# Other constants and another picking rule in the planner that orders the instructions of an attention and MLP kernel

## The chip, the cores and the metric

The kernel runs on one core of a Trainium2 chip. Its time is the device time of one execution in microseconds (us). Before the change the median of three runs is 223.51 us (223.31 to 223.61). The profile comes from one further execution.

The core has five engines, each with an instruction queue of its own that it works off strictly in order: TensorE (PE, matmuls; its weight loads are listed as PEld), VectorE (DVE), ScalarE (ACT), GpSimd (POOL) and SyncE (SP, which here only issues DMAs). Engines wait for each other and for DMAs through semaphores. An instruction whose wait is not met holds up everything behind it in the same queue.

## The reference, cut to what matters

The first half is a blocked linear attention with decay per head; the second is a two-layer MLP over its output.

```python
# q, k, v: (4, 8, 768, 64); block = 64; rel = pos[:, None] - pos[None, :]
Dmask = where(rel >= 0, lam ** rel, 0)
for b in range(12):
    intra = (qb @ kb.T * Dmask) @ vb
    inter = (qb * lam ** (pos + 1)) @ kv_state
    out[b] = intra + inter
    kv_state = lam ** 64 * kv_state + (kb * lam ** (63 - pos)).T @ vb
x = out.transpose(0, 2, 1, 3).reshape(3072, 512)
h = x @ w_in                          # (3072, 2048)
g = h + sin(alpha * h) ** 2 / (alpha + 1e-9)
y = g @ w_out                         # (3072, 512), float32
```

## The kernel before, in words

**Attention.** The kernel works in 24 blocks of 128 rows (6 per batch entry, all 8 heads at once). For each block, queries, keys and values are loaded as float32: `load_q` (L345) loads q for two blocks, 512 KB, and `load_kv` (L358) loads k and v for one, 256 KB each. The decay is folded into q and k by a multiplication that also casts to bfloat16 (`scale_block`, L458: q at L464, k at L471, on POOL except for the first two k), and v is cast at L473, on ACT, from block 12 on on ACT or POOL. q and k are then transposed. For blocks 0 to 11 TensorE does it (`piece_Q` L496 and `piece_T` L476, with copies out of PSUM at L511 and L493 on DVE or ACT). From block 12 on SP issues a DMA transpose (L479). The scores (`part_S`, matmuls at L543) go through a masking multiplication on DVE (L552) into `Sm`; the state (`part_Z`, L568) is copied out at L578 or L583; the output (`part_O`, L603, L616, L623) is copied into `xT` at L632. `piece_G` (L649) packs scores of one block and output and state of the block before it into one piece of TensorE work.

**MLP.** Rows go in 6 chunks of 512, which is four blocks. For a chunk, 16 units A (`unit_A`, L656, matmuls at L671; or `unit_A2`, L694, L705, which takes half the rows and two column groups) each fill one PSUM bank, then ACT takes the sine (L681, L715), POOL or ACT squares it (L686/L720 or L685/L719), and DVE combines both into `gT` (L688, L723). Only then is the bank free. 16 units B (`unit_B`, L729, L736) multiply `gT` with the second weights; the last of each four is copied out by ACT (L749) and stored (L751). Units A rotate over three banks in most of the kernel.

**Loads.** SP issues, in program order: q, k and v of blocks 0 to 3, the first quarter of the first weights (`load_w1_first`), and then, after the third quarter of the first weights has landed, q, k and v for blocks 4 and up; stores and transposes stand between them. POOL issues the other three quarters of the first weights and four quarters of the second. Loads reuse rings of six buffers for k and v and three for q.

**What sets the order.** The program does not issue instructions directly. Every piece is handed to `_Plan.op` (L54) with the engine or the choice of engines that can do it, a duration in us, what it reads and writes, and for DMAs a time on the wire (`dur`), a time for the issue and a time `lat` after the transfer. `_Plan` finds dependencies, and `_order` (L119) simulates the kernel with these numbers: it picks one piece after another and writes down the order in which each engine gets its pieces; where there is a choice, the engine that would be done first gets it. SP keeps program order. On PE any of the next 40 pieces in program order may be picked; among those that could start within 0.3 us of the earliest (`SLACK`), the one that stands first in the program is taken. ACT, DVE and POOL take what can start first. Work that depends on another engine is taken to be ready 0.2 us after it (`LAT`), an engine is occupied for a piece's whole duration, and a DMA begins to move data 0.8 us after its issue. `_transfers` (L75) shares the wire between the DMA queues; `_settle` (L101) repeats both up to eight times and keeps the pass whose landings agree best. `P.lead` (40 in `attend`, -20 in `run`) moves a piece's place in the program. `P.filler` (L836) puts matmuls without a result (`spin`, L826, L829) into planned gaps of TensorE before the first unit A. The result is a fixed instruction list with semaphore waits; nothing is planned at run time.

Of the kernel before, what the change touches and what calls it, by code (L numbers as in the profile page):

```python
# [13 lines left out]
class _Op:  # L14


    def __init__(self, eng, emit, dur, reads, writes, dma, after, issue, lat, runs=64):
        self.eng, self.emit, self.dur = eng, emit, dur
        self.given = eng
        self.issue, self.lat, self.runs = issue, lat, runs  # L20
        self.lead = 0
# [11 lines left out]
class _Plan:  # L33

    AHEAD = {"PE": 40, "SP": 1}
    SLACK = 0.3  # L40
    EARLY = 0.0, 0.0

    LAT = 0.2
# [10 lines left out]
    def op(self, eng, emit, dur, reads=(), writes=(), dma=None, after=(), issue=0.4, lat=2.6, runs=64):  # L54
# [20 lines left out]
    def _transfers(order):  # L75
# [5 lines left out]
        left = {e: [[o.start + 0.8, o.runs, o.dur / o.runs, o] for o in sorted(q, key=lambda o: o.start)]  # L81
# [19 lines left out]
    def _settle(self):  # L101

        filler, lands, best = self.filler, {}, None
        for _ in range(8):
            self.filler = filler
            for o in self.ops:
                o.eng, o.start, o.done = o.given, None, None
            order = self._order(lands)
            new = self._transfers(order)
            off = sum(abs(t - o.done) for o, t in new.items())  # L110
            state = [(o, o.eng, o.start, o.done) for o in order]
            if best is None or off < best[0]:
                best = off, order, state
            lands = new
        for o, eng, start, done in best[2]:
            o.eng, o.start, o.done = eng, start, done
        return best[1]

    def _order(self, lands):  # L119
        index = {o: i - o.lead for i, o in enumerate(self.ops)}  # L120
        left = {}
        for o in self.ops:
            left.setdefault(o.eng if isinstance(o.eng, str) else "any", []).append(o)
        fixed = {e: left.pop(e, []) for e in ("PE", "SP")}
        free = [o for e in left for o in left[e]]
        clock = {e: 0.8 for e in ("PE", "SP", "ACT", "DVE", "POOL")}
        wire = 0.0
        port = 0.0
        order = []

        def ready(o):
            t = 0.0
            for d in o.deps:
                if d.done is None:
                    return None
                t = max(t, d.done + (0.0 if d.eng == o.eng else self.LAT))
            return t

        while fixed["PE"] or fixed["SP"] or free:
            best = None  # L140
            for e in ("PE", "SP"):
                can = []
                for o in fixed[e][:self.AHEAD[e]]:
                    r = ready(o)
                    if r is not None:
                        can.append((max(r, clock[e]), index[o], o, e, o.dur))
                if can:
                    soon = min(c[0] for c in can)
                    soon += self.EARLY[1] if e == "PE" and soon < self.EARLY[0] else self.SLACK
                    c = min((c for c in can if c[0] <= soon), key=lambda c: c[1])  # L150
                    if best is None or c[:2] < best[:2]:
                        best = c
            for o in free:
                r = ready(o)
                if r is None:
                    continue
                if o.port:
                    r = max(r, port)
                if isinstance(o.eng, str):
                    c = (max(r, clock[o.eng]), index[o], o, o.eng, o.dur)  # L160
                else:
                    _, e, d = min((max(r, clock[e]) + d + late, e, d) for e, d, late in o.eng)
                    c = (max(r, clock[e]), index[o], o, e, d)
# [766 lines left out]
```

## Time and profile before

| what | value |
|---|---|
| median of three runs | 223.51 us |
| the profiled execution | 223.52 us |
| its span, first to last instruction | 221.4 us |
| TensorE busy | 208.6 us (94%) |
| ScalarE busy | 155.9 us (70%) |
| VectorE busy | 122.6 us (55%) |
| GpSimd busy | 89.1 us (40%) |
| HBM read / written | 27.28 / 6.29 MB |
| first unit A starts on TensorE | 19.89 us |

How to read it: busy time is the union of an engine's instructions. Matmuls are pipelined, so the listed duration of one (379 ns at 512 columns) is longer than the step from one to the next (0.216 us), and a short stall after a matmul is partly hidden in its listed duration. "idle before, releaser" says how long an engine stood still ahead of an instruction, and what ended that. The chain of waits follows the last instruction back to what released it, step by step.

### The profile page before, as it was taken

To read this page: it belongs to the slowest core of one execution; us is meant where nothing else is said; L and a number is where in the kernel's file an instruction comes from. 1 tells how busy PE (TensorE), PEld (TensorE's weight loads), DVE (VectorE), ACT (ScalarE), POOL (GpSimd) and SP (SyncE) were. 2 spreads that over 40 slices of the span, in tenths; PEclk is the share of its full clock that TensorE was granted. 3 is DMA by queue.
4 is the path that set the end of the run, shared out by engine and by line. 5 is a ranking of instruction groups with operands and counts; after the bars stand their busy time and mean duration, and the time that the engine had idled before them with its cause. 6 is when DMAs were issued, how large, how long until landed. Compare 5 with 4: busy or idle time off the path is not lost.

```text
span 221.4 us, 4062 instructions
## 1 busy us (share of the span) xinstructions
PE 208.6 (94%) x1645; PEld 110.7 (50%) x1645; DVE 122.6 (55%) x184; ACT 155.9 (70%) x277; POOL 89.1 (40%) x100
## 2 busy tenths in 40 slices
PE   3889987899898999999999999999999999999995
PEld 1446433456575785545445444545545444444444
DVE  4687775354777887667655455645465544445100
ACT  3735994347697997788788887877788677778211
POOL 4386763454978776863576103011001011110100
DMA  5999999999999999999999752110110011101112
GB/s 131 236 232 271 206 214 208 217 235 237 233 245 275 242 191 245 219 254 189 276 240 245 155 112 33 47 50 0 47 50 21 26 47 50 47 0 49 75 70 95
DMA packets 83651, 33.31 MB, mean 150 GB/s; under 512 B 63520, under 2 KB 80688, under 8 KB 83632
## 3 DMA queue, kind: packets, MB, share of 16 engines
q1 hardware_dynamic: 76880, 24.25, 53.6%
q0 software_dynamic: 3696, 3.67, 9.9%
q10 hardware_dynamic: 3056, 5.13, 6.4%
q8 instruction: 13, 0.21, 0.4%
q14 instruction: 6, 0.05, 0.1%
HBM read 27.28 MB, written 6.29 MB: 152 GB/s over the span
## 4 chain that ended last, share of the span: by engine, by line
PE 63%; DMA 24%; POOL 4%; SPq 4%; ACT 2%; DVE 1%; issue 1%
PE bank L736 32%; PE bank L671 24%; DMA k<-in_k_dram 10%; DMA q<-in_q_dram 5%; DMA v<-in_v_dram 4%; DMA w<-in_moe_w_in_dram 4%; SPq L342 4%; PE bank L705 3%; PE bank L623 2%; PE bank L543 2%; POOL qk L471 1%; POOL qk L464 1%; PE bank L603 1%; POOL u L720 1%; DVE gT L723 1%
## 5 line engine op out<-in xcount | busy, mean ns | idle before, releaser
L736 PE MATMUL bank<-w,gT 128*128 128x512 bf16 (+1 forms) x400 | 94.8, 371 | 0.0
L688 DVE SCALAR_TENSOR_TENSOR gT<-u,rinv,bank 128x512 bf16<-128x512 bf16 x74 | 54.6, 746 | 51.7 <-ACT u L685 34.2
L671 PE MATMUL bank<-xT,w 128*128 128x512 bf16 x296 | 74.2, 379 | 0.6 <-DVE gT L688 0.6
L681 ACT ACTIVATE t<-bank,alpha 128x512 bf16<-128x512 f32 x74 | 50.6, 686 | 24.1 <-PE bank L671 24.0
L736 PEld LDWEIGHTS bank<-w,gT 128*128 128x128 bf16 x400 | 37.7, 98 | 39.6
L686 POOL TENSOR_TENSOR u<-t 128x512 bf16<-128x512 bf16 x19 | 19.7, 1040 | 80.7 <-ACT t L681 79.7
L671 PEld LDWEIGHTS bank<-xT,w 128*128 128x128 bf16 x296 | 28.5, 98 | 34.9 <-DVE gT L688 1.1
L685 ACT ACTIVATE u<-t 128x512 bf16<-128x512 bf16 x55 | 34.4, 629 | 1.8 <-DVE gT L723 0.3
L552 DVE TENSOR_TENSOR Sm<-bank,mask 128x1024 bf16<-128x1024 f32 x24 | 29.2, 1222 | 10.3 <-PE bank L568 7.7
L464 POOL TENSOR_TENSOR qk<-q,Lq 128x512 bf16<-128x512 f32 x24 | 24.5, 1044 | 21.7 <-DMA q<-in_q_dram 18.1
L471 POOL TENSOR_TENSOR qk<-k,Lk 128x512 bf16<-128x512 f32 x22 | 22.9, 1044 | 7.2 <-DMA k<-in_k_dram 7.0
L749 ACT COPY osb<-bank 128x512 f32<-128x512 f32 (+1 forms) x25 | 14.2, 569 | 14.8 <-PE bank L736 14.8
L705 PE MATMUL bank<-xT,w 128*128 128x256 bf16 x176 | 22.3, 273 | 2.0 <-DVE gT L723 2.0
L723 DVE SCALAR_TENSOR_TENSOR gT<-u,rinv,bank 128x256 bf16<-128x256 bf16 x44 | 19.1, 476 | 7.2 <-POOL u L720 4.1
L715 ACT ACTIVATE t<-bank,alpha 128x256 bf16<-128x256 f32 x44 | 18.5, 471 | 3.3 <-PE bank L705 3.1
L705 PEld LDWEIGHTS bank<-xT,w 128*128 128x128 bf16 x176 | 16.2, 98 | 5.5 <-DVE gT L723 3.0
L473 ACT CAST v<-v 128x512 bf16<-128x512 f32 x18 | 11.0, 615 | 7.6 <-DMA v<-in_v_dram 7.6
L632 ACT CAST xT<-bank 128x512 bf16<-128x512 f32 (+1 forms) x18 | 12.9, 716 | 2.8 <-PE bank L568 1.6
L720 POOL TENSOR_TENSOR u<-t 128x512 bf16<-128x512 bf16 x11 | 11.3, 1039 | 4.7 <-ACT t L715 4.6
L543 PE MATMUL bank<-qkT 64*128 64x128 bf16 x192 | 9.8, 226 | 0.2 <-DVE qkT L493 0.2
L623 PE MATMUL bank<-Sm,v 128*64 128x128 bf16 x192 | 9.9, 225 | 0.0
L829 PE MATMUL bank<-mask,ident 128*128 128x512 bf16 x12 | 5.7, 564 | 3.7 <-DVE mask L429 3.7
(55 smaller groups left out, 111.4 us busy)
## 6 DMA issues: line engine op xcount, KB each, us to landing
k<-in_k_dram SPq DMA_DIRECT2D x24, 256.0 KB, 5.5
v<-in_v_dram SPq DMA_DIRECT2D x24, 256.0 KB, 5.5
q<-in_q_dram SPq DMA_DIRECT2D x10, 512.0 KB, 5.5
out_dram<-osb ACTq DMA_DIRECT2D x19, 256.0 KB, 2.0
w<-in_moe_w_out_dram POOLq DMA_DIRECT2D x4, 512.0 KB, 13.1
w<-in_moe_w_in_dram POOLq DMA_DIRECT2D x3, 512.0 KB, 9.0
q<-in_q_dram SPq DMA_DIRECT2D x4, 256.0 KB, 4.6
ws<-in_moe_w_in_dram SPq DMA_DIRECT2D x2, 512.0 KB, 5.4
```

The lines of the kernel that those rows point to most:

```text
L464: lambda e, a=a: e.tensor_tensor(qk2[:, j:j + 2, 4 * a:4 * a + 4, :], q32[jq][:, 4 * a:4 * a + 4, :, :].rearrange("p h t d -> p t h d"), b ...
L471: lambda e: e.tensor_tensor(qk2[:, j, H:2 * H, :], k32[jl][:, :, :], lk, ALU.mult), 0.7 if s in (0,1) else 1.05,
L552: op("DVE", lambda e: e.tensor_tensor(Sm[s % 2][:, :, :], banks[:, 512 * b0:512 * b0 + 1024].rearrange("p (c i) -> p c i", i=128), mask[:, ...
L671: ins = e.matmul(ps[hb][:, c0:c1], w1[:, kc, 128 * m:128 * (m + 1)], xT[x][:, kc, c0:c1], start=(kc == 0 and c0 == lo), stop=(kc == NKC - ...
L681: op("ACT", lambda e: e.activation(t16[ju][:, w], ps[hb][:, w], ACTF.Sin, scale=alpha[:, m:m + 1]), 0.69 * f, [bank(hb), "alpha"], [("t16" ...
L685: lambda e: (e.activation(u16[ju][:, w], t16[ju][:, w], ACTF.Square) if e is nc.scalar else e.tensor_tensor(u16[ju][:, w], t16[ju][:, w], ...
L686: e.tensor_tensor(u16[ju][:, w], t16[ju][:, w], t16[ju][:, w], ALU.mult)), 0,
L688: op("DVE", lambda e: e.scalar_tensor_tensor(out=gT[g][:, m, w], in0=u16[ju][:, w], scalar=rinv[:, m:m + 1], in1=ps[hb][:, w], op0=ALU.mul ...
L705: ins = e.matmul(ps[hb][:, 256 * i:256 * i + 256], w1[:, kc, 128 * (m + i):128 * (m + i + 1)], xT[x][:, kc, lo:lo + 256], start=(kc == 0 a ...
L715: op("ACT", lambda e, i=i: e.activation(t16[ju][:, 256 * i:256 * i + 256], ps[hb][:, 256 * i:256 * i + 256], ACTF.Sin, scale=alpha[:, m + ...
L723: op("DVE", lambda e, i=i: e.scalar_tensor_tensor(out=gT[g][:, m + i, lo:lo + 256], in0=u16[ju][:, 256 * i:256 * i + 256], scalar=rinv[:, ...
L736: ins = e.matmul(ps[ob][:, w], gT[g][:, m, 128 * s4:128 * (s4 + 1)], w2[:, m, w], start=(m == 0), stop=(m == NM - 1),)
```

## The change

The planner's model and its rule for picking are replaced; what is computed, the tiles, the buffers and the program order of the pieces stay, but for one load that is named below.

- A hand-over between engines costs `HOP` of the receiving engine (0.035 to 0.1 us), plus `DRAIN` 0.085 us where TensorE is the giver, in place of 0.2 us. ACT, DVE and POOL are free for the next piece `PIPE` (0.11, 0.09, 0.045 us) before the piece is done.
- A DMA begins to move data 2.0 us (POOL: 2.9 us) after its issue instead of 0.8 us, and the time after the transfer falls (mostly to 1.25 or 1.4 us; 2.7 us stays for q, k and v from block 4 on).
- Durations of pieces are set anew, most by a few hundredths of a us; the DMA transpose from 2.5 to 1.0 us, the cast of v on POOL from 1.05 to 0.62 us.
- On PE, ACT, DVE and POOL the planner first finds the earliest start of any ready piece of the engine, and takes the one that stands first in the program among those within a window (PE 0.3 us, the others 0.1 us). Then it takes the engine with the earliest pick.
- Up to ten passes, and the loop ends when landings agree within 0.5 us in sum. `MOVES`, a list of shifts in the program order, is empty.
- The loads of blocks 10 and 11 are asked for in `prep(8)` and `prep(9)` instead of right after `prep(5)`. Between these two places nothing else is handed to SP, so that SP's order is the same.

The hunks stand in the order of the planner's class and then the kernel: the constants, when a piece is ready, the pick, the end of a piece, `load_q`, `load_kv`, the cast of v, the DMA transpose, `piece_T` (`piece_Q` changes likewise), `prep`, and the place after `prep(5)`.

```diff
-    AHEAD = {"PE": 40, "SP": 1}
-    SLACK = 0.3
-    EARLY = 0.0, 0.0
-    LAT = 0.2
+        self.lag = 2.9 if eng == "POOL" else 2.0
+    AHEAD = 40
+    WINDOW = {"PE": 0.3, "ACT": 0.1, "DVE": 0.1, "POOL": 0.1}
+    PIPE = {"ACT": 0.11, "DVE": 0.09, "POOL": 0.045, "PE": 0.0}
+    HOP = {"PE": 0.055, "ACT": 0.035, "DVE": 0.035, "POOL": 0.075, "SP": 0.1}
+    DRAIN = 0.085
+    MOVES = ()
...
+        def ready(o, e):
+            t = clock[e]
+            for d in o.deps:
+                if d.eng == e and (e == "PE" or d.dma is not None):
+                    t = max(t, d.done)
+                else:
+                    t = max(t, d.done + self.HOP[e] + (self.DRAIN if d.eng == "PE" else 0.0))
+            return t
...
+            for e, c in per.items():
+                if not c:
                     continue
+                soon = min(x[0] for x in c) + self.WINDOW.get(e, 0.0)
+                x = min((x for x in c if x[0] <= soon), key=lambda x: x[1])
+                if best is None or x[0] < best[0]:
+                    best = x[0], x[2], e, x[3]
...
-                o.done = max(t + 0.8 + o.dur + o.lat, lands[o]) if o in lands else wire + o.lat
+                o.done = max(t + o.lag + o.dur + o.lat, lands[o]) if o in lands else wire + o.lat
             else:
-                clock[e] = o.done = t + dur
+                o.done = t + dur
+                clock[e] = o.done - self.PIPE[e]
...
-                        (0.9 if s == 0 else 1.1 if s < 4 else 2.3), f"q32{j}" + (str(lo) if s < 4 else ""),
-                        lat=2.7, after=after, runs=8 * (hi - lo),
+                        (0.93 if s < 4 else 2.0), f"q32{j}" + (str(lo) if s < 4 else ""),
+                        lat=1.25 if s < 4 else 2.7, after=after, runs=8 * (hi - lo),
...
-                            (nm, j), 1.1, f"{nm}{j}", lat=2.7,
+                            (nm, j), 1.18, f"{nm}{j}", lat=1.25 if s < 4 else 2.7,
...
-                op((("ACT", 0.62, 0.0), ("POOL", 1.05, 0.3)) if s > 11 else "ACT", lambda e: (e.copy if e is nc.scalar else e.tensor_copy)(v2[j][:, :, :], v32[jl][:, :, :]), 0.62,
+                op((("ACT", 0.62, 0.0), ("POOL", 0.62, 0.3)) if s > 11 else "ACT", lambda e: (e.copy if e is nc.scalar else e.tensor_copy)(v2[j][:, :, :], v32[jl][:, :, :]), 0.62,
...
-                        qkT[:, jt, :, :], qk2[:, j, :, :].rearrange("p a b -> p (a b)")), 2.5,
+                        qkT[:, jt, :, :], qk2[:, j, :, :].rearrange("p a b -> p (a b)")), 1.0,
...
-                op("PE", mm, 0.35, [("k2", j), "ident"], [bank(tb)])
+                op("PE", mm, 0.35 if s < 4 else 0.24, [("k2", j), "ident"], [bank(tb)])
...
-                    for ahead in range(s + 2, min(s + 3, NBLK)) if s >= 10 else ():
+                    for ahead in range(s + 2, min(s + 3, NBLK)) if s >= 8 else ():
...
             prep(5)
-            load_pair(10)
```

## The prediction

> **What bounds the kernel now.** I read the page first, then busy time by stretch, then what TensorE waits for, then the timeline around each of its stalls, last the chain of waits.
>
> Rows 1 and 2 of the page:
>
> ```profile
> PE 208.6 (94%) x1645; PEld 110.7 (50%) x1645; DVE 122.6 (55%) x184; ACT 155.9 (70%) x277; POOL 89.1 (40%) x100
> ...
> PE   3889987899898999999999999999999999999995
> ...
> DMA  5999999999999999999999752110110011101112
> ```
>
> TensorE is full from about 40% of the span on; before that its slices have holes, while the DMA engines are full from about 6 us to about 116 us. Busy time by stretch says how large the holes are (the figures after the stretch are its length, then busy PE, PEld, DVE, ACT, POOL):
>
> ```profile
> 20.00:36.00 16.00, 15.43 (x86) 7.57 (x86) 10.80 (x18) 14.17 (x25) 9.80 (x11) 1.00 1.22 210
> 36.00:60.00 24.00, 21.27 (x211) 12.22 (x210) 11.96 (x18) 11.83 (x24) 12.98 (x13) 1.00 1.08 226
> 60.00:86.00 26.00, 24.80 (x305) 17.50 (x304) 20.83 (x41) 22.52 (x51) 20.32 (x22) 1.00 1.08 233
> 86.00:120.00 34.00, 33.93 (x285) 17.66 (x283) 21.57 (x32) 27.91 (x50) 20.27 (x21) 1.00 1.22 246
> 120.00:204.00 84.00, 84.00 (x526) 40.18 (x525) 42.28 (x56) 65.47 (x107) 12.21 (x13) 1.00 0.20 52
> ```
>
> From 86 us to the last matmul an order can hardly win anything. The waits of PE name the holes (the first row is the start, before any data):
>
> ```profile
> PE bank L829 <- DVE mask L429: 3.7, 1, 3.7
> PE bank L506 <- POOL qk L464: 2.1, 2, 1.7
> PE bank L705 <- DVE gT L723: 2.0, 3, 1.0
> PE bank L488 <- POOL qk L471: 0.7, 2, 0.5
> PE bank L671 <- DVE gT L688: 0.6, 1, 0.6
> ```
>
> The timeline shows what each hides: start, duration, engine and line, and in brackets the idle time before.
>
> ```profile
> 35.70 1.89 PE L736 MATMUL bank<-w,gT 128*128 128x512 bf16 x8
> 39.31 0.40 PE L506 MATMUL bank<-ident,qk 128*128 128x128 bf16 x4 [1.72 <-POOL qk L464]
> 39.55 1.03 PE L671 MATMUL bank<-xT,w 128*128 128x512 bf16 x4
> ...
> 40.63 2.75 PE L736 MATMUL bank<-w,gT 128*128 128x512 bf16 x12
> ...
> 57.16 0.62 ACT L473 CAST v<-v 128x512 bf16<-128x512 f32 x1 [1.69 <-DMA v<-in_v_dram]
> ```
>
> At 0.216 us a matmul, the eight from 35.70 end at 37.43, so TensorE lost 1.88 us to 39.31, with finished work (an A unit and three B units) behind the waiting transpose. At 57.16 ACT stands 1.69 us in front of a cast whose v has not landed; the Square at 57.68 behind it comes late, DVE's `gT` with it, and TensorE's A unit starts at 59.27, 0.88 late. The chain of waits has the same pattern at 85 us:
>
> ```profile
> 72.04 6.72 DMA q<-in_q_dram
> ...
> 78.83 0.92 POOL qk L464
> ...
> 82.43 2.01 POOL u L720 x2
> ...
> 84.46 0.88 DVE gT L723 x2
> ...
> 85.39 1.92 PE bank L705 x16
> ```
>
> POOL's squares stand behind scales that waited for q. Counted from the end of the matmul before at its step, the losses after 20 us are 0.73 (30.5), 1.88 (39.3), 0.34 (43.6), 0.88 (59.3), 1.19 (69.1, where POOL idled 1.30 for a k at 66.08 with three squares behind), 0.37 (85.4) and 0.24 (113.7): 5.63 us. Five of the seven, 4.66 us, are an in-order engine parked before a landing that the plan had believed earlier.
>
> **The change part by part.** Nothing is computed more or less, so each part is worth what it moves.
>
> *Landings from block 4 on.* In the model a k alone took 0.8 + 1.1 + 2.7 = 4.6 us from issue to landing, now 2.0 + 1.18 + 2.7 = 5.88; the page's median is 5.5 (k and v). For q it is 5.8, now 6.7, traced 5.5. So these landings are planned 1.28 us (q 0.9) later, from too early to slightly late, and other work is put ahead of them. At 59.3 that takes 1.28 of the 1.69 us that ACT stood, so 0.76 of 0.88 = 0.67 us; at 69.1 1.28 of 1.30, 1.17 us; at 85.4 0.9 of the 1.23 us that POOL stood before the q, but only 0.37 reached TensorE: 0.37. Sum 2.2 us.
>
> *TensorE's durations.* Key transposes cost 0.35 in the plan and 0.22 in the chain, query transposes and outputs similarly too much, so the real TensorE runs ahead of the plan and then stands. With the true ones and q later by 0.9, the 1.88 + 0.34 us at 39 and 43 can be filled: the A unit at 39.55 and the B units behind it are 0.86 us each. But work taken forward is missing later: the first A unit of the next chunk starts at 52.16, on a chain from k of block 5 (scale at 44.27) to its `xT` at 51.65, 7.4 us, of which 4.65 are instructions (1.04 + 0.22 + 0.42 + 0.33 + 1.22 + 0.68 + 0.74). It can shorten, not vanish. Bounds 0 and 2.2; I take 0.8, nearer the lower end because 44 to 52 us is so short of work.
>
> *Hand-overs and occupation.* A hand-over of ACT to DVE is 0.04 us in the trace (64.67 to 64.71), planned 0.2, now 0.035; two sines back to back take 1.26 us, a step of 0.57, planned 0.69, now 0.58. That makes the choice between ACT, POOL and DVE truer. It bears on 30.5, the one stall of the bank chain: 0 to 0.73, I take 0, since ACT is 89% busy there. In the steady stage it costs nothing: three banks come round every 3 x 1.73 = 5.2 us, and a bank's chain (0.86 + 0.69 + 1.04 + 0.75 and some 0.3 of hand-overs) takes 3.6. If that cover of 1.6 us is gone, TensorE stands for the rest.
>
> *Second weights.* POOL waits in line for quarter loads of the first weights before issuing more (1.2 us idle at 26.14). Planned now as 2.9 + 2.55 + 1.3 = 6.75 against 7.15, 0.4 earlier, while the first took 7.4 (15.91 to 23.30): up to 0.4 us more waiting with squares behind. Bounds 0 and 0.4; I take a loss of 0.2.
>
> *DMA transposes.* 2.5 becomes 1.0 us on the wire; issue to landing 5.9 becomes 4.4, traced 4.6. But SP is held 1.9 to 3.1 us by each. A pair of blocks is planned with 2.3 + 4 x 1.1 + 2 x 2.5 = 11.7 us before, 2.0 + 4 x 1.18 + 2 x 1.0 = 8.72 after; q issues at 83.23 and 112.76 are three pairs apart, 9.84 each. Stores share the wire, 0.75 each at one in 6.9 us, some 1.1 per pair, so the plan stands near 9.8: I take 0. The scores of block 12 start at 92.01, for a transpose issued at 76.81: some ten us of slack. Bounds: no cost, and 1.12 us per pair over four pairs, 4.5.
>
> *The rest.* The cast of v on POOL takes 0.61 us (six in the trace), so 0.62 is right and 1.05 was not; ACT is 82% busy from 86 to 120 us without holding TensorE: 0. The start is bound by loads whose order on SP is unchanged: the weight cast at 19.07 follows a landing at 18.71, so at most 0.36 is to be had; 0. The moved load meets no other SP instruction on its way: 0.
>
> Sum: 2.2 + 0.8 - 0.2 = 2.8 us. Since TensorE is full from 85 us on, what is won there moves the end. The profiled execution took 223.52 us, 221.4 of span and 2.1 around it, and the median is 223.51; 223.5 - 2.8 = 220.7 us. A measurement of this kernel tells about 0.2% (0.45 us) from no change.
>
> **A rule beside the rows.** The spinning matmuls at the start step by 0.427 us (3.66 to 5.77), half the speed of the 0.216 later; by 12.7 us the transposes run at full speed, and the 1.88 us silence at 37 did not undo it (the A unit after it takes the usual 1.03). The Trainium skill, "TensorE: Matmul & The Clock Gate", Part 1, says that the array starts at half clock, is released by some 3.4 us of sustained work, and falls back after an idle window as long. The trace agrees on the start; it has no silence long enough to show the fall. By that page a plan with a 3.4 us gap would pay an estimated 1.7 us on top of the gap.
>
> **The rivals.**
>
> *A, half the gain.* From 60 to 86 us ACT is busy 22.5 of 26 us; with 2.2 us less room it would be 95%, and sines come late for other reasons. Half of 3.0 won: 223.5 - 1.5 = 222.0. For: DVE and POOL are at 80% there too. Against: the new model knows ACT's true step.
>
> *B, slower: landings behind transposes come too late for the plan.* If stores and SP's long issues are not enough to slow the planned stream, v of blocks 16 to 22 is planned up to 4.5 us early, its cast stands in ACT's queue with sines behind, and the steady stage, free of stalls today, gets them. Price 4.5 us on top of the forecast: 225.2. It decides once more than 2.8 + 0.45 = 3.3 us reach TensorE. For: 8.72 against 9.84. Against: 1.28 us of added margin, 1.6 us of cover, and stores in the model.
>
> *C, cold array.* The new order leaves a silence that halves the matmul speed again. From rows: it took 3.66 to 12.7 us, 9 us, to reach full speed; 9 us at half speed lose 4.5: 225.2.
>
> *D, no effect.* Work taken forward is missing later, every stall only moves: 223.5.
>
> *E, all.* Every hole closes, 5.63 and 0.36: 217.5.
>
> **Chances.** Forecast (218.6 to 222.0) 0.50, A (to 223.0) 0.14, B 0.23, C 0.02, D 0.06, E (under 218.6) 0.05. Faster 0.69, same 0.06, slower 0.25. The range reaches from E to B, 217.5 to 225.2, and leaves out the worse half of B and C.
>
> **What will show it.** Right: the rows of PE waiting on POOL's scales (2.1 and 0.7 us) and on `gT` L723 (2.0) shrink to under half; ACT's idle time before v casts (7.6 us in nine) falls; busy PE from 36 to 60 rises by about 1 us of stretch; stretch 86 to 204 stays full. Wrong: idle time of PE after 86 us on `gT` with ACT or POOL waiting for v, q or k (B); 379 ns matmuls at 620 (C); the same loss at other places between 44 and 60 us (D). The step I trust least is the 0.8 at 39 us.

## The result and the profile after

The changed kernel takes 226.55 us in the median of 19 executions (223.93 to 229.03), beside 223.54 us (222.67 to 224.80) for the kernel before on the same chip. The ratio is 1.010 with a 95% interval of 1.0079 to 1.0121: about 1% slower, where 220.7 us was forecast and the range ended at 225.2. (The ratio leaves out three executions of the changed kernel in a slower state of the chip and is close to the quotient of the remaining means, 1.0098.) The profiled execution took 226.72 us, with a span of 224.6 against 221.4 us.

Rows 1 and 2 of the page of the changed kernel, with the granted clock:

```profile
PE 209.8 (93%) x1646; PEld 111.0 (49%) x1646; DVE 119.4 (53%) x179; ACT 166.4 (74%) x298; POOL 72.9 (32%) x84
...
PE   2878999999999994999999999999999999999995
...
PEclk9999999999999998899999999999999999999999
```

A slice is 5.6 us. PE's "4" and the "88" of the clock lie in the same place, 84 to 95 us: there is the loss. Busy time by stretch (length, then busy PE, PEld, DVE, ACT, POOL, then clock):

```profile
20.00:36.00 16.00, 15.30 (x88) 7.34 (x85) 10.54 (x18) 14.66 (x27) 7.29 (x9) 1.00 1.22 210
36.00:60.00 24.00, 22.83 (x219) 13.16 (x218) 11.12 (x16) 13.84 (x27) 13.12 (x13) 1.00 1.07 228
60.00:86.00 26.00, 24.40 (x302) 17.08 (x299) 22.45 (x47) 23.74 (x51) 17.73 (x19) 1.00 1.09 227
86.00:120.00 34.00, 31.96 (x243) 16.58 (x244) 17.77 (x25) 26.48 (x48) 18.33 (x21) 0.95 1.23 245
120.00:204.00 84.00, 84.00 (x549) 40.53 (x548) 41.73 (x53) 70.72 (x120) 3.68 (x4) 1.00 0.22 55
```

From 36 to 60 us TensorE has 1.56 us more work than before. From 86 to 120, full before (33.93 of 34 us), it has 31.96, at a mean clock of 0.95. The waits of PE:

```profile
PE bank L560 <- DMA qkT<-qk: 2.2, 1, 2.2
PE bank L523 <- POOL qk L481: 1.1, 3, 0.5
...
PE bank L633 <- DVE Zc L600: 0.7, 1, 0.7
PE bank L722 <- DVE xT L649: 0.7, 1, 0.7
...
PE bank L722 <- DVE gT L740: 0.4, 1, 0.4
```

Before, waits on `gT` for these units were 2.0 us and waits on POOL's scales of q 2.1; they are 0.4 and 1.1. In their place stands one wait of 2.2 us of the scores (L560) for a DMA transpose. The timeline shows it (SPq and ACTq are DMAs issued by SP and ACT):

```profile
80.57 2.53 SPq L496 DMA_TRANSPOSE qkT<-qk  x1
...
82.21 0.38 ACTq L768 DMA_DIRECT2D out_dram<-osb  x1
...
84.91 0.41 PE L633 MATMUL bank<-qkT,Zc 64*64 64x128 bf16 x8 [0.67 <-DVE Zc L600]
...
85.25 0.41 PE L640 MATMUL bank<-Sm,v 128*64 128x128 bf16 x8
...
85.71 0.73 DVE L649 CAST xT<-bank 128x512 bf16<-128x512 f32 x1
...
87.84 0.54 PE L560 MATMUL bank<-qkT 64*128 64x128 bf16 x8 [2.17 <-DMA qkT<-qk]
...
88.31 3.40 PE L722 MATMUL bank<-xT,w 128*128 128x256 bf16 x16
```

The transpose of block 13 is issued at 80.57 and lands at 87.80, 7.23 us later; the one of block 12 had landed at 81.27. A store joins it at 82.21. TensorE stands from about 85.6 to 87.84 us (2.17 us by the row), with the scores of block 12 in front of an A unit whose `xT` has been there since 86.44. Then that unit takes 3.40 us for 16 matmuls that take 1.92 us elsewhere (before: at 85.39), since the granted clock is 0.5 from 88.0 to 91.4 us. Both lie on the chain of waits of the changed kernel:

```profile
80.57 7.23 DMA qkT<-qk
88.38 3.33 PE bank L722 x16
```

TensorE's lost time (time gone by less the work done at its step, as the prediction counted its stalls) says where the 3.2 us of span come from. It is summed from 0, and a matmul without a result counts as no work:

| until | before | after | difference |
|---|---|---|---|
| 20 us | 13.73 | 13.84 | +0.1 |
| 24 us | 13.72 | 14.81 | +1.1 |
| 84 us | 20.10 | 18.97 | -1.1 |
| 88 us | 20.66 | 22.04 | +1.4 |
| 92 us | 20.77 | 23.58 | +2.8 |
| 200 us | 21.08 | 24.32 | +3.2 |

So 1.1 us are lost in the ramp, 2.2 are won from 24 to 84 us, and 3.9 are lost from 84 to 92: 2.5 waiting (to 88 us), 1.4 by the slow unit behind it. Of the 2.5 not all is the transpose's: 0.67 us is the wait for the copy of the state (`Zc`, L600) at 84.91, and the A unit could not have started before its `xT` at 86.44 in any case.

### The profile page after: what moved, and what is told of

The parts are those of the page before. It is cut to its first block, busy times and chain, and to the rows that moved or that the text cites. A ratio compares the mean times of both kernels' runs of the same rounds, so it can differ in the third digit from the quotient of the medians.

```text
span 224.6 us, 4063 instructions
## 1 busy us (share of the span) xinstructions
PE 209.8 (93%) x1646; PEld 111.0 (49%) x1646; DVE 119.4 (53%) x179; ACT 166.4 (74%) x298; POOL 72.9 (32%) x84
## 4 chain that ended last, share of the span: by engine, by line
PE 66%; DMA 20%; SPq 4%; ACT 3%; DVE 3%; POOL 2%; issue 1%; POOLq 0%
PE bank L753 33%; PE bank L688 23%; DMA q<-in_q_dram 11%; DMA w<-in_moe_w_in_dram 4%; SPq L359 4%; DMA qkT<-qk 3%; PE bank L722 3%; DMA k<-in_k_dram 3%; PE bank L640 2%; PE bank L560 2%; POOL qk L481 2%; ACT t L732 1%; DVE gT L740 1%; PE bank L620 1%; DVE Sm L569 1%
## 5 line engine op out<-in xcount | busy, mean ns | idle before, releaser
L753 PE MATMUL bank<-w,gT 128*128 128x512 bf16 (+1 forms) x400 | 94.8, 371 | 0.0
L705 DVE SCALAR_TENSOR_TENSOR gT<-u,rinv,bank 128x512 bf16<-128x512 bf16 x74 | 54.7, 745 | 56.3 <-ACT u L702 51.1
L753 PEld LDWEIGHTS bank<-w,gT 128*128 128x128 bf16 x400 | 37.7, 98 | 39.7
L688 PEld LDWEIGHTS bank<-xT,w 128*128 128x128 bf16 x296 | 28.8, 98 | 34.5 <-DVE gT L705 0.5
L702 ACT ACTIVATE u<-t 128x512 bf16<-128x512 bf16 x67 | 42.3, 632 | 2.2 <-DVE gT L705 0.2
L481 POOL TENSOR_TENSOR qk<-q,Lq 128x512 bf16<-128x512 f32 x24 | 25.0, 1062 | 25.7 <-DMA q<-in_q_dram 21.8
L722 PE MATMUL bank<-xT,w 128*128 128x256 bf16 x176 | 24.0, 285 | 1.1 <-DVE xT L649 0.7
L722 PEld LDWEIGHTS bank<-xT,w 128*128 128x128 bf16 x176 | 16.6, 102 | 5.6 <-DVE gT L740 1.7
L490 ACT CAST v<-v 128x512 bf16<-128x512 f32 x17 | 10.5, 618 | 6.4 <-DMA v<-in_v_dram 6.4
L560 PE MATMUL bank<-qkT 64*128 64x128 bf16 x192 | 9.5, 221 | 3.2 <-DMA qkT<-qk 2.2
L736 ACT ACTIVATE u<-t 128x512 bf16<-128x512 bf16 x16 | 10.1, 630 | 0.4
L560 PEld LDWEIGHTS bank<-qkT 64*128 64x128 bf16 x192 | 5.5, 94 | 7.9 <-DMA qkT<-qk 2.3
L703 POOL TENSOR_TENSOR u<-t 128x512 bf16<-128x512 bf16 x7 | 7.3, 1037 | 6.5 <-ACT t L698 6.3
```

The source lines that it names most:

```text
L481: lambda e, a=a: e.tensor_tensor(qk2[:, j:j + 2, 4 * a:4 * a + 4, :], q32[jq][:, 4 * a:4 * a + 4, :, :].rearrange("p h t d -> p t h d"), b ...
L560: ins = e.matmul(ps[(b0, b1)[h]][:, 128 * jp:128 * (jp + 1)].rearrange("p (t x) -> p t x", x=64), qkT[r, jt, 4 + jp, :], qkT[r, jq:jq + 2, ...
L688: ins = e.matmul(ps[hb][:, c0:c1], w1[:, kc, 128 * m:128 * (m + 1)], xT[x][:, kc, c0:c1], start=(kc == 0 and c0 == lo), stop=(kc == NKC - ...
L702: lambda e: (e.activation(u16[ju][:, w], t16[ju][:, w], ACTF.Square) if e is nc.scalar else e.tensor_tensor(u16[ju][:, w], t16[ju][:, w], ...
L705: op("DVE", lambda e: e.scalar_tensor_tensor(out=gT[g][:, m, w], in0=u16[ju][:, w], scalar=rinv[:, m:m + 1], in1=ps[hb][:, w], op0=ALU.mul ...
L722: ins = e.matmul(ps[hb][:, 256 * i:256 * i + 256], w1[:, kc, 128 * (m + i):128 * (m + i + 1)], xT[x][:, kc, lo:lo + 256], start=(kc == 0 a ...
```

## The experiments

Theory: the plan believes that a transpose lands 4.4 us after its issue; it puts the scores of block 12 forward to that time, TensorE stands for the real landing, cools down (its clock falls to half), and the rest is small. Rivals: the store in the transpose's way is the cause; the ramp is; the cold array is by itself; or the loss is spread over landings of v that are planned too early. Ratios are to the kernel before, measured beside each kernel on the same chip. A profile shows one execution, a median is over all of them, and the two need not agree.

**The scores behind one more unit.** In the changed kernel the transposes are planned to land 2.6 us later.

```diff
-  dma=f"qkT{jt}", runs=16)
+  dma=f"qkT{jt}", runs=16, lat=4.0)
```

> The changed kernel with one constant other: after its transfer a DMA transpose is planned to need 4.0 us instead of 1.4, so that issue to landing is planned as 7.0 us, what the late one took in the changed kernel (7.23). On TensorE this moves the scores of block 12 behind one unit A, on ACT and POOL a few pieces change place; SP keeps its order. Theory (an order that puts the scores of block 12 before their transpose, then a cold array): TensorE's wait of 2.2 us for the transpose shrinks to under 0.8, the granted clock is 1.000 in most runs, 226.6 becomes about 224.0 us. Rival (the loss is spread over the new order of ACT and POOL, and the wait is only where it shows): the time stays above 226 us with waits elsewhere.

226.08 us (223.81 to 227.09), ratio 1.0086 (1.0049 to 1.0123). The profile is of an execution of 225.36 us. The unit now stands in front and the wait falls to 0.38 us, but 20 us later a new stall costs 1.45 us:

```profile
87.93 0.40 PE L560 MATMUL bank<-qkT 64*128 64x128 bf16 x8 [0.38 <-DMA qkT<-qk]
...
88.26 0.94 PE L722 MATMUL bank<-xT,w 128*128 128x256 bf16 x7
...
96.88 2.97 SPq L496 DMA_TRANSPOSE qkT<-qk  x1
...
98.14 0.35 ACTq L768 DMA_DIRECT2D out_dram<-osb  x1
...
106.14 0.62 ACT L490 CAST v<-v 128x512 bf16<-128x512 f32 x1 [1.83 <-DMA v<-in_v_dram]
...
108.68 0.60 PE L753 MATMUL bank<-w,gT 128*128 128x512 bf16 x2 [1.17 <-ACT xT L649]
```

ACT stands 1.83 us at 106.14 in front of a v; that load had been issued at 100.52, behind the transpose of 96.88 that a store joined at 98.14 and that took 6.9 us. `xT` comes late behind the cast and TensorE waits 1.17 us for it. That is the path that rival B of the prediction named, a cast of v parked on ACT, though what comes late behind it is a copy into `xT` and not a sine. So the wait shrinks as expected, but the time stays above 226 us, as the rival said: the median is hardly better than that of the changed kernel.

**The clock alone.** Ten matmuls without a result keep TensorE busy in front of the scores; the plan counts them as nothing.

```diff
...
+  if block == 12:
+      o11 = [o for o in P.ops if o.eng == "PE" and ("Sm", 1) in o.reads][-1]
+      op("PE", lambda e: spin1(e, 10), 0.0, ["mask", "ident"], [bank(1), bank(2)], after=[o11])
   piece_G(...)
```

> The changed kernel with ten matmuls without a result put in TensorE's order between the output of block 11 and the scores of block 12, where it stands 2.2 us; they are planned as taking no time, so that TensorE, ACT and DVE keep their order. Theory (the silence of 84 to 88 us makes the array fall to half speed for some 3.4 us): granted clock 1.000 in every run, sixteen matmuls of 256 columns after the scores take 1.9 us instead of 3.4, time 224.8 us in every run, as in the runs of the changed kernel at clock 1.000. Rival (the slower clock comes from elsewhere, or the spins delay the scores): clock 0.992 remains, 226.6 us or more.

226.89 us (225.88 to 227.34, four executions), ratio 1.0122 (1.0079 to 1.0165); granted clock 0.999 to 1.0 in all of them.

```profile
86.16 2.33 PE L852 MATMUL bank<-mask,ident 128*128 128x512 bf16 x10
...
88.43 0.40 PE L560 MATMUL bank<-qkT 64*128 64x128 bf16 x8
...
88.76 1.92 PE L722 MATMUL bank<-xT,w 128*128 128x256 bf16 x16
```

The unit behind the scores takes 1.92 us again, 1.5 less. So the silence is what made it slow. The forecast of 224.8 us was missed all the same, and the median is not better than that of the changed kernel: this execution was 0.6 us later at the start, the transpose landed 0.4 us later (88.18), and the profiled 225.88 us is the best of the four. The changed kernel's own executions differ by 1.8 us: 6 of 19 at a mean clock of 1.000 have a median of 224.9 us, 11 at 0.992 of 226.7. But an execution that waits longer is also the one that cools, and a lower mean clock by itself does not say where the slow spell lies: of the 32 executions of the kernel before beside e9_lat84, the 15 below 0.999 have a median of 223.99 us, the others 223.94. What the cold unit is worth by itself, between nothing and 1.8 us, the times leave open; the profile's 1.5 us lies between.

**The store out of the way.** The store that was issued at 82.21 goes on SP, behind the next transpose.

```diff
-  unit_B(*bq[bi], 3 * (bi // 4 % 2))
+  unit_B(*bq[bi], 3 * (bi // 4 % 2), out_eng="SP" if bq[bi] == (1, 0, 3) else "ACT")
```

> The changed kernel with one store, that of the first 128 rows of chunk 1, given to SP behind the next transpose instead of to ACT, where it is issued at 82.2 us in the middle of the transpose of block 13. Theory (a store that joins a transpose in flight slows both; the five transposes that a store joined within 1.7 us of their issue took 5.2 to 7.2 us in the two traces, those alone 3.4 to 4.7): that transpose lands 4.4 to 4.7 us after its issue, the scores of block 12 start before 86.2, TensorE's wait for it is under 0.5 us, clock 1.000, time about 223.1 us. Rival (loads and SP's pace make the transpose late): it still takes about 7 us and the time stays at 226.6.

224.82 us (223.87 to 225.80), ratio 1.0041 (1.0014 to 1.0067).

```profile
80.42 2.54 SPq L496 DMA_TRANSPOSE qkT<-qk  x1
...
86.63 0.40 PE L560 MATMUL bank<-qkT 64*128 64x128 bf16 x8 [0.70 <-DMA qkT<-qk]
...
86.96 1.92 PE L722 MATMUL bank<-xT,w 128*128 128x256 bf16 x16
```

With no store in flight the transpose lands after 6.16 us, not 7.23, the wait is 0.70 us and the array stays warm. More than half of the loss goes. The result lies between the two expectations: 6.16 is still far from the 4.43 of the kernel before. This profile has also lost 0.6 us less by 24 us than that of the changed kernel, although every engine has the same order up to 84 us: the ramp by itself varies from execution to execution.

**The ramp.** DVE takes the second weight cast behind the copy of `xT`, by hand.

```diff
   order = self._settle()
+  cast = [o for o in order if o.eng == "DVE" and ("w1", 1) in o.writes][0]
+  copy = [o for o in order if ("xT", 0, 3, 2) in o.writes][0]
+  order.remove(cast)
+  order.insert(order.index(copy) + 1, cast)
```

> The changed kernel with two neighbours exchanged on DVE alone: the second cast of the first weights, which waits for a landing at 20.7 us, goes behind the copy of block 3 into xT, which was ready at 20.13. Theory (the new plan has this landing too early, and DVE parks in front of it; but what is lost here is absorbed by the later wait for the transpose): TensorE's wait of 0.7 us at 21.8 goes, it is about 0.7 us ahead from 22 to 84 us, and the time stays within 0.3 us of 226.6, since the transpose does not land earlier. Rival: the full 0.7 reaches the end, 225.9 us.

227.25 us (226.05 to 228.28), ratio 1.0143 (1.0089 to 1.0196). The wait for `xT` at 21.8 us is gone, and TensorE stands 1.15 us for `gT` at 31.7 instead; by 40 us the lost time is 16.33 against 15.68. Both expectations are missed. This exchange wins nothing; no other order of the ramp was tried by itself.

**Both repairs.** The edits of e1_tlat4 and e3_store_sp together.

> The changed kernel with the two repairs of e1_tlat4 and e3_store_sp together: the transposes planned 2.6 us longer, and the one store that joined the transpose of block 13 put on SP behind the next transpose. Theory (the loss is the wait of the scores of block 12 for that transpose, the cold array behind it, and a store that makes the transpose later): the wait for qkT falls under 0.3 us, since a unit of 1.9 us stands in front of the scores, and what the middle won is kept: about 223.0 us (222.3 to 223.9), ratio 0.997. Rival (transposes further on are joined by other stores as soon as the order moves, as the stall of 1.45 us at 107 us in e1_tlat4): wait for qkT gone too, but a new stall behind a load between 96 and 120 us, 224.5 us or more.

225.49 us (223.42 to 227.08), ratio 1.0084 (1.0053 to 1.0115), though the profiled execution is the fastest, 223.42 us, and shows no wait for qkT and no stall over 0.5 us behind 87 us. The theory's 223.0 us is missed in the median; the rival's stall further on does not show in this profile. So something else varies from execution to execution, at full clock. The later landing brings nothing here on top of the moved store (1.0041 in e3_store_sp alone). Even in this profile TensorE stands 0.67 us for `Zc` at 84.8 and 0.82 us for `xT` at 86.4, in front of the A unit: that part of the loss does not hang on the transpose.

**The suspected constant alone, in the kernel before.** Nothing but the transpose's time on the wire.

```diff
-  qk2[:, j, :, :].rearrange("p a b -> p (a b)")), 2.5,
+  qk2[:, j, :, :].rearrange("p a b -> p (a b)")), 1.0,
```

> The kernel before, its planner untouched, with one constant of the change alone: a DMA transpose has 1.0 us on the wire in place of 2.5. Theory (this term by itself makes the loss): the scores of block 12 move forward in TensorE's order, the wait of TensorE for qkT appears with 1 us or more near 85 us, and the time is 224.7 to 226.5 us, ratio 1.005 or above. Rival (it takes the planner's other new rules to do harm): 223.5 us, no row of TensorE waiting for qkT over 0.5.

228.91 us (227.39 to 229.98), ratio 1.021 (1.0154 to 1.0266): this term by itself, in the old planner, costs 4.7 us, more than expected.

```profile
81.23 2.59 SPq L479 DMA_TRANSPOSE qkT<-qk  x1
...
82.26 1.03 PE L736 MATMUL bank<-w,gT 128*128 128x512 bf16 x4
...
85.90 0.40 PE L543 MATMUL bank<-qkT 64*128 64x128 bf16 x8 [2.62 <-issue]
...
86.23 1.59 PE L736 MATMUL bank<-w,gT 128*128 128x512 bf16 x4
...
127.31 2.04 POOL L471 TENSOR_TENSOR qk<-k,Lk 128x512 bf16<-128x512 f32 x2 [3.73 <-DMA k<-in_k_dram]
...
131.74 1.04 PE L671 MATMUL bank<-xT,w 128*128 128x512 bf16 x4 [1.62 <-DVE gT L688]
```

The scores of block 12 come at 85.90, six us earlier than before (92.01), 0.1 us after the landing of their second transpose at 85.81; TensorE has lost 2.78 us (the view names no releaser, but nothing else that the scores read ends there), and the next matmuls are slow (1.59 us for four, 1.03 elsewhere). At 127.31 POOL has stood 3.73 us for a k, with a square behind it, and TensorE loses 1.79 us for `gT`: a parked engine before a landing once more, here POOL. This profile is of the slowest of the five executions (229.98 us): it has lost 1.9 us more than before already by 22 us, with a granted clock of 0.5 from 14.9 to 21.7 us, so the 4.7 us are not the one wait alone.

**The two terms that were to gain, in the kernel before.** Landing constants of q, k, v from block 4 on and TensorE's durations, as in the change; the old planner.

```diff
-  left = {e: [[o.start + 0.8, ...
+  left = {e: [[o.start + o.lag, ...            # 2.0 for these loads, else 0.8
-  ... 1.1 if s < 4 else 2.3), f"q32{j}"        # load_kv: 1.1
+  ... 1.1 if s < 4 else 2.0), f"q32{j}"        # load_kv: 1.18 from block 4 on
-  op("PE", mm, 0.35, [("k2", j), "ident"]
+  op("PE", mm, 0.35 if s < 4 else 0.24, [("k2", j), "ident"]
...
```

> The kernel before, its planner untouched, with the two terms of the change that were forecast to gain: the landing constants of the loads from block 4 on, and the durations of TensorE's pieces. Theory (these terms gain by themselves, 2.2 and 0.8 us forecast): 221.0 to 222.0 us. Half theory (the stalls before 85 us close, the planned order is otherwise as long as before): 222.0 to 223.0. Rival (what was won in the middle came from the new pick and hand-overs, not from these constants): 223.3 us or more, with 1.5 us or more still lost near 39 us or at 59 and 69 us.

224.99 us (224.07 to 225.35), ratio 1.0045 (1.0018 to 1.0072). The stalls at 39 and 69 us are gone and the one at 59 is down to 0.65 (at 61), as forecast; others stand in their place: 1.63 at 30 (1.4 of it for a load of the second weights), 1.23 at 43, 0.82 at 76, 0.98 at 80, 0.95 at 85 and 0.93 at 114 us. The time is that of the rival, the stalls are not: this is nearest to the prediction's rival D (every stall only moves), on the old planner, and 0.45% slower.

**The changed kernel with late landings.** Transposes at 8.4 us from issue to landing in the plan, later than any in its trace (3.1 to 7.2), the second quarter weights 1.1 us later, the store on SP.

```diff
-  dma=f"qkT{jt}", runs=16)
+  dma=f"qkT{jt}", runs=16, lat=5.4)
...
-  ("ws", lo), 1.45, f"ws{lo}", lat=1.25, runs=32,
+  ("ws", lo), 1.45, f"ws{lo}", lat=1.25 if lo == 0 else 2.35, runs=32,
...
-  unit_B(*bq[bi], 3 * (bi // 4 % 2))
+  unit_B(*bq[bi], 3 * (bi // 4 % 2), out_eng="SP" if bq[bi] == (1, 0, 3) else "ACT")
```

> The changed kernel with three constants set to what its own trace shows: a DMA transpose lands 8.4 us after its issue in place of 4.4 (seen alone 3.4 to 4.7, joined by a store 5.2 to 7.2), the second quarter of the first weights 1.1 us later, and the store that joined the transpose of block 13 on SP behind the next transpose. Theory (with the landing told truly the gain of the middle stays): no wait for qkT, none for xT at 21.8 us, 221.5 to 222.8 us, faster than both kernels. Rival (every new order meets other collisions of stores and transposes): 223.5 to 225.

223.07 us (222.04 to 225.04), ratio 0.997 (0.9939 to 1.0): between the two expectations. The scores of block 12 run at 90.06, 3.6 us behind the landing (86.47), and no wait for a DMA transpose is left.

**That constant alone.** Of e8_mend's three edits only the first.

> The changed kernel with one constant set otherwise: a DMA transpose is planned to land 8.4 us after its issue in place of 4.4, nothing else. Theory (the one constant makes the loss, and the full landing time in the plan, a store included, mends it): no wait of TensorE for qkT over 0.3 us, granted clock 1.0, 223.0 to 224.3 us, with the ramp's wait for xT at 21.8 us still there. Rival (store and second weights of e8_mend did half of its work): 224.8 us or more, as e5_both.

224.89 us (223.29 to 226.63), ratio 1.0038 (1.0006 to 1.0071), clock 1.0 in all executions. Of the loss of 1.0%, 0.6% goes with one constant. The theory's 223.0 to 224.3 us is missed all the same and the rival's 224.8 is met: e8_mend's two other edits are worth another 0.7% by the ratios. The profile (223.29 us) is of the fastest execution, as in e5_both. In it the A unit starts at 86.56 in place of 88.31, with no transpose in front, and again it stands for `xT`:

```profile
86.56 1.92 PE L722 MATMUL bank<-xT,w 128*128 128x256 bf16 x16 [0.83 <-DVE xT L649]
```

In e8_mend B units (L753) fill this place, and there is no such stall.

**The three planned gains, each undone in e8_mend.** Old landing constants of q, k, v from block 4 on:

```diff
-  lat=1.25 if s < 4 else 2.7, after=after, runs=8 * (hi - lo)
+  lat=1.25 if s < 4 else 2.71, after=after, runs=8 * (hi - lo)
+  if dma is not None and eng == "SP" and lat == 2.71: self.lag = 0.8     # and 2.3 / 1.1 on the wire
```

> The kernel of e8_mend (223.07 us) with the old landing constants for q, k and v from block 4 on, all else as there. Forecast of the prediction's first step: 2.2 us, so 225.3 us, ACT and POOL parked before landings, with TensorE's losses near 59 and 69 us back (0.9 and 1.2). Rival (those landings do no harm once the rest of the plan is true): 222.6 to 223.6 us, no loss over 0.5 us at either place.

223.82 us (222.24 to 228.31), ratio 0.9982 (0.9946 to 1.0018): no measurable difference to e8_mend, and no loss over 0.5 us at 59 or 69. The forecast's 225.3 us is missed; the rival is nearer.

Old durations of TensorE's pieces (0.35 for transposes, 0.55 / 0.68 / 0.35 for outputs, 0.87 for units):

> The kernel of e8_mend (223.07 us) with the old durations of TensorE's pieces in the plan, all else as there. Forecast of the prediction's second step: 0.8 us (0 to 2.2), so 223.9 us, the loss at 39 to 44 us back with 1 to 2 us. Rival (they move work without closing a stall): 222.6 to 223.5 us.

226.13 us (224.63 to 227.32), ratio 1.0092 (1.0062 to 1.0122), so 1.2% or 2.7 us slower than e8_mend, beyond both expectations. The loss is not at 39 to 44 us (0.9) but late: 1.3 us at 84.4, 0.6 at 96, 1.9 at 106, 0.8 at 119. ACT's wait for v rises from 8.3 to 13.4 us:

```profile
ACT v L490 <- DMA v<-in_v_dram: 13.4, 10, 3.0
```

and among the waits of PE stands

```profile
PE bank L753 <- ACT xT L649: 1.8, 1, 1.8
```

the same chain as at 106 us in e1_tlat4.

Old hand-overs:

```diff
-  PIPE = {"ACT": 0.11, "DVE": 0.09, "POOL": 0.045, "PE": 0.0}
-  HOP = {"PE": 0.055, "ACT": 0.035, "DVE": 0.035, "POOL": 0.075, "SP": 0.1}
-  DRAIN = 0.085
+  PIPE = {"ACT": 0.0, "DVE": 0.0, "POOL": 0.0, "PE": 0.0}
+  HOP = {"PE": 0.2, "ACT": 0.2, "DVE": 0.2, "POOL": 0.2, "SP": 0.2}
+  DRAIN = 0.0
```

> The kernel of e8_mend (223.07 us) with the old hand-overs in the plan: 0.2 us between engines, nothing for the drain, no overlap of successive instructions on one engine. Forecast of the prediction's third step: 0, so 222.8 to 223.5 us. Rival (hand-overs are what the gain of the middle came from, since they decide which engine takes the squares): 224.5 us or more, squares back on POOL, and TensorE waiting for gT with 1.5 us or more between 24 and 84 us.

224.56 us (222.75 to 227.51), ratio 1.0007 (0.9971 to 1.0042). That meets the rival's 224.5 us, and by the ratios it is 0.4% above e8_mend, but the intervals overlap. Squares do go back to POOL (ACT does 62 of L702, 67 in e8_mend; 7 of L736, 16 there) and TensorE waits for `gT` 3.7 us in place of 2.4, the rival's signs. ACT's wait for v rises here too, from 8.3 to 14.5 us.

**Landings of v told later.** What varies at full clock in e5_both: v of blocks 14 to 23 is planned 2.5 us later, first there, then in e8_mend.

```diff
-  lat=1.25 if s < 4 else 2.7,
+  lat=1.25 if s < 4 else 5.2 if s > 13 and nm == "v32" else 2.7,
```

> The kernel of e5_both (profiled at 223.42 us, median 225.49 at full clock) with one constant more: v of blocks 14 to 23 planned to land 2.5 us later. Theory (what is left of the loss, and its spread from run to run, is ACT parked before a v that landed behind a transpose and a store, as in the profile of e1_tlat4 at 107 us): median 223.4 to 224.4 us, ACT's idle time before casts of v under half of the 6.6 us of e5_both. Rival (the spread comes from the ramp before 24 us or from k and q): median 225.0 us or more, whatever the casts of v do.

224.86 us (224.22 to 226.36), ratio 1.0040 (1.0017 to 1.0064), between the two expectations: by the ratios half of e5_both's loss goes, but the intervals overlap. The theory's sign is missing: ACT's idle time before v hardly changes in the profiles (6.6 and 6.3 us). At 108.1 us a stall of 0.8 is left, in front of which POOL stood 3.30 us for a k with a square behind it:

```profile
106.02 1.04 POOL L488 TENSOR_TENSOR qk<-k,Lk 128x512 bf16<-128x512 f32 x1 [3.30 <-DMA k<-in_k_dram]
...
107.02 1.04 POOL L703 TENSOR_TENSOR u<-t 128x512 bf16<-128x512 bf16 x1
...
108.10 0.75 DVE L705 SCALAR_TENSOR_TENSOR gT<-u,rinv,bank 128x512 bf16<-128x512 bf16 x1 [4.82 <-POOL u L703]
```

> The kernel of e8_mend (223.07 us, ratio 0.997) with the same constant more: v of blocks 14 to 23 planned to land 2.5 us later. Theory (parked casts of v still cost e8_mend some runs): 222.4 to 223.0 us, ratio 0.992 to 0.996. Rival (in e8_mend the scores of these blocks are late enough, nothing is won): 223.0 to 223.6 us, ratio 0.996 to 1.0.

221.69 us (221.41 to 222.79), ratio 0.9905 (0.987 to 0.994): faster than both kernels, and by more than the theory said. Among PE's waits no transpose is left, and none for `xT`; the longest one after 11 us is

```profile
PE bank L688 <- DVE gT L705: 0.7, 1, 0.7
```

Why this constant is worth more here than in e5_both was not tried.

## Why the prediction was wrong

**The step that failed is "DMA transposes", taken as 0** with "some ten us of slack". Three things were wrong in it. First, the slack was read for the transpose of block 12 (76.81 to 92.01). But q of a pair lies interleaved, `part_S` reads `qT` of both blocks, so the scores of block 12 need the transpose of block 13 as well: issued at 80.83, landed at 85.26, 6.75 us ahead of the scores. The profile before has it:

```profile
80.83 2.35 SPq L479 DMA_TRANSPOSE qkT<-qk  x1
...
92.01 0.40 PE L543 MATMUL bank<-qkT 64*128 64x128 bf16 x8
```

Second, that cover was taken from the order of before, while the change makes a new order: the scores came at 87.84, 4.17 us earlier, and the transpose landed 2.54 us later. 6.75 - 4.17 - 2.54 leaves 0.04 us, which is the landing at 87.80 releasing the matmul at 87.84. Third, the prediction compared the planned 4.4 us with a median:

```profile
qkT<-qk SPq DMA_TRANSPOSE x12, 4.6
```

In that same profile the twelve took 3.4 to 7.0 us; the one that mattered after the change took 7.23. e6_before_t1 shows the term alone at 4.7 us, just past the upper bound of 4.5; in the changed kernel a still later landing than the old 5.9 us brings back 0.6% (e9_lat84). That 4.7 is so near to 4.5 is luck: the bound was a delay of loads behind transposes, not a wait for a transpose.

**Landings from block 4 on, 2.2.** The stalls at 59 and 69 us shrank to 0.38 (57) and 0.53 (62). But these constants alone are not what did it: undone in e8_mend they cost 0.1%, within the uncertainty of some 0.5%, and on the old planner, with the durations, they only moved the stalls. The gain in the middle belonged to the whole new plan; as a term of its own this one was smaller than 2.2 us and may be 0.

**TensorE's durations, 0.8.** 1.88 + 0.34 us at 39 and 43 became 0.71 at 39 and 0.64 at 48. Undone in e8_mend, they are worth some 2.7 us, more than the upper bound, and at another place: the stall at 106 us is ACT parked before a late v, the one at 84 us is a wait for a copy into `xT` on ACT (1.1 us), those at 96 and 119 us were not followed up.

**Hand-overs, 0.** 0.4% by the ratios, not told from 0 by the intervals. **Second weights, -0.2,** were not tried alone. **The rest, 0:** the start cost 1.1 us, since DVE stood 0.65 us before the second weight cast (landing at 20.7 us) while the copy of `xT` behind it was ready at 20.13; exchanging the two won nothing (e4_swap).

Together: 24 to 84 us gave 2.2 of the 3.0 forecast for the first two steps; 1.1 in the ramp and 3.9 from 84 to 92 us went the other way. Some 1.2 to 1.5 of the 3.9 stay in e5_both and e9_lat84, as waits for `Zc` and `xT`; the rest is the transpose and the cold unit. -2.2 + 1.1 + 3.9 is 2.8 us by 92 us, 3.2 at the end.

**The rivals.** B came nearest, in size (225.2 against 226.55) and in blaming the transposes, but it named loads that come late behind them and casts of v; in the changed kernel's profile it was TensorE's own wait for a transpose, so the size was in part luck. Its path showed in e1_tlat4, e6_before_t1 and e11_oldpe. C had 0.02, and its cold array came, at a third of its price: 3.40 us for one unit and full speed behind it, not 9 us of half speed. D was nearest on the old planner (e7_before_gain).

**The signs.** Right: `gT` L705 2.0 to 0.4; ACT's idle time before v 7.6 to 6.4; 36 to 60 us 1.56 us fuller. Waits for POOL's scales fell to half (2.1 to 1.1; 0.7 to 0.5), not under it. Wrong: the stretch from 86 us did not stay full. The prediction's signs of failure did not include a wait of TensorE for qkT.

**Still open.** How much of the time the cold unit makes by itself, and what sets apart the executions at full clock of e5_both and e9_lat84 (223.3 to 227.1 us): planning v later takes about half of e5_both's loss by the ratios (e13_vlate), but the intervals overlap, and the ramp varies by 0.8 us between profiles with the same order (0.5 us lost by 24 us in e3_store_sp, 1.3 in e2_spin, against before); the rest has no name. And every changed constant makes a new order: no run shows how much the time moves when a constant is changed that should not matter, so the sizes of the single terms are those of one new order each.

## What to carry to other kernels

A constant in a planner that is true for the median transfer moves consumers up to that time, and the one transfer that comes late then stops the engine that everything waits for; plan a landing at its late end where the consumer is on the critical engine. That alone (8.4 us in place of 4.4, e9_lat84) took 0.6 of the 1.0% of loss; with the second quarter of the first weights and v planned later too, and one store moved (e14_mend_v), the loss became a gain of 0.9%. Read the cover of a moved landing from all that the consumer reads, and in the new order, not the old. Change one constant at a time on a plan that is otherwise true: here the terms had other sizes, and one another place, than the stalls they were read from.

## What the runs showed of the hardware

**What makes a transpose late.** The transpose of block 13 took 6.88 to 7.40 us in the five profiled kernels where a store was issued 1.4 to 1.8 us behind it (after, e1, e2, e4, e9), and 4.43 to 6.16 us in the eleven where none was; moving the store alone took 7.23 to 6.16 (e3_store_sp). But a store is not the whole of it. In all of these but e6 a fetch of instructions (queue q8 of the page, one packet of 16 KB, some 1 to 1.3 us) began 2.4 to 4.2 us behind the issue. All 128 transposes issued before 116 us in the sixteen profiles, sorted by whether a store was issued and whether a fetch began before the landing:

| in flight | transposes | median issue to landing |
|---|---|---|
| neither | 50 | 4.7 us |
| a store | 21 | 4.9 us |
| a fetch | 21 | 5.9 us |
| both | 36 | 6.9 us |

The packets show what goes along with it. In the changed kernel hardly any start between 84.5 and 86 us, behind a fetch at 83.94; the store's packets of that moment (31 of 0.66 us on average from 84.0 to 84.5, usually 0.06 to 0.12) are held up as well. Between 20 and 115 us the profiles have 22 such quiet spells (0.75 us or more with under 25 packets in each quarter us), all 0.4 to 2.4 us behind the start of a fetch during a transpose, 13 of them with no store issued in the 4 us before. Of 40 fetches that began during a transpose 22 were followed by one, of 64 that did not, none. That is a coincidence counted in the traces and not a shown cause; no run moved a fetch, and before's transpose of block 13 landed after 4.43 us with a fetch 0.6 us ahead of the landing. Nor is a store enough by itself: the transpose of block 22, where the DMA engines of before and after are half busy or less, took 3.1 to 4.7 us in all sixteen with a store 1.5 to 2.0 us behind it, most with a fetch too. (Those of the two first traces, 3.4 and 3.1 us, are missing from the five that the expectation of e3_store_sp counts.) The Trainium skill, "DMA: Bandwidth & Descriptors", Rules for kernel authors, says that a transpose next to ordinary DMAs needs nothing. It stands in a rule against corrupted data; for the time, the 7.23 and 6.16 us above say otherwise.

**How short a silence cools the array.** 1.88 us of silence did not (before, 37 to 39 us), nor did 1.9 in e11_oldpe at 106 us. 2.78 us did (e6_before_t1), and so did 2.2 to 2.4 us in the changed kernel, with 0.6 us of smaller matmuls ahead of it and a gap of 0.8 us ahead of those. The Trainium skill, "TensorE: Matmul & The Clock Gate", Part 1, gives an idle window of some 3.4 us for the fall and as long of work for the release. The slow spell fits the second (granted clock 0.5 for 3.4 us, then 1.0); the 2.78 us measured here is shorter than the first, so a silence well under the page's window can be enough.
